# Pooled attention and MLP on one core: keys tiled by head pair, with the leftovers in 32-column matmul tiles

## The chip, the cores and the metric

The kernel runs on one core of a Trainium2 chip. The metric is the device time of one execution in microseconds. Before the change the median of 6 runs is 308.84 us (308.72 to 309.54).

A core has engines that run side by side, each through its own list of instructions in order: TensorE (PE; its weight loads are listed as PEld), VectorE (DVE), ScalarE (ACT), GpSimd (POOL) and SyncE (SP), which here issues transfers only. ACT and POOL issue transfers too. All transfers share 16 DMA engines. TensorE writes its results to PSUM, from which DVE and ACT copy them to the on-chip memory SBUF.

## What is computed

Eight batches of eight heads, 576 tokens, head size 64. Keys and values are averaged over groups of 8 tokens, so a head has 72 pooled keys; the attention output of all heads, 512 wide, goes through an MLP with 2048 hidden units.

```python
batch, n_heads, seq, head_dim = (8, 8, 576, 64)
n_tokens, d_model, d_ff = (4608, 512, 2048)

def _attn_ref(q, k, v):
    pool = 8
    Sp = S // pool                                   # 72
    k_p = k.reshape(B, H, Sp, pool, D).mean(axis=3)
    v_p = v.reshape(B, H, Sp, pool, D).mean(axis=3)
    scores = scale * np.matmul(q, k_p.transpose(0, 1, 3, 2))
    scores = scores - np.max(scores, axis=-1, keepdims=True)
    attn = np.exp(scores)
    attn = attn / (np.sum(attn, axis=-1, keepdims=True) + 1e-09)
    return np.matmul(attn, v_p).astype(np.float32)

def _moe_ref(x, w_in, w_out):
    h = x @ w_in
    g = h - np.tanh(h)
    return (g @ w_out).astype(np.float32)
```

## The kernel before

The order of work is written out by hand: every engine runs its instructions in the order in which the program issues them, and waits where an input is not there yet.

**Keys.** The 8 x 72 = 576 pooled rows of a batch (all heads) are cut into tiles of 128 rows: four full ones and one of 64 (`NT = 5`). `load_rows` (L96) loads tiles 0 to 3 in one transfer on SP and the last in another. `pool_k` (L171) sums each row's 8 tokens in three additions, 8 to 4, 4 to 2, 2 to 1, and writes the sum twice, side by side, into `kd`. `k_transpose` (L212) turns `kd` with matmuls against the identity; because the sum stands there twice, a head's keys appear on partitions 0 to 63 and again on 64 to 127. They are copied into `KB`, which holds for each of the four head pairs a block of all 5 x 128 key columns: an even head on partitions 0 to 63, an odd head on 64 to 127, zeros elsewhere. A tile of 128 rows holds parts of two or three heads, so its scores need the sum over the one or two pairs that it touches (`PAIRS`, L242): 8 matmuls for 5 tiles, or 16 in the two halves of 288 tokens of `scores` (L244). `scores_wide` (L269) does 512 tokens at once, `scores_tail` (L278) the last 64. ACT takes the exponential into `E`.

**Values.** `pool_v` (L193) sums values and multiplies them by a mask into `VB`, with three slots per tile for the heads that the tile may touch; a 65th column per slot gives the softmax's denominator. `av_half` (L296) multiplies `E` by `VB` for four heads: three matmuls of 130, 195 and 65 columns (`XM`, L264) into one PSUM tile `x_ps`; DVE takes the reciprocal of the denominators and multiplies (L311, L312) into `x_sb`. `x_pe_transpose` (L335) turns that on TensorE into `xT`; from batch 2 on a transfer on SP does it (L329).

**MLP.** Tokens go in 9 groups of 512. Per group 16 units of `mlp_h` (four matmuls L380, tanh on ACT L391, subtraction on DVE L393), then 16 units of `mlp_o` (four matmuls L408 each). The attention of batch g+1 is put between the `mlp_o` units of group g: `k_transpose` after unit 0, scores after units 1 to 5, `x_ps` after units 7, 8, 9, 10 and 12. POOL does `pool_k`, `pool_v` and the cast of q ahead of it; SP loads the batch after that while unit 3 of `mlp_h` runs.

**Start (batch 0).** SP loads k in three pieces (tiles 0 and 1, tile 4, tiles 2 and 3), ACT issues q's, POOL v's as bf16 into `v_bf` and then the weights `w1b` (four pieces) and `w2b`. `k_turn` (L547) and `v_pe_pool` (L586) are batch 0's own forms: DVE sums the keys, TensorE sums the values by eight accumulating matmuls against the identity. `warm_pe(n)` puts n spare matmuls into TensorE's list. `av_half` runs for heads 0 to 3 of all four token blocks and then for heads 4 to 7.

**Batch 1** stands between the `mlp_o` units u of group 0 (L679 to L701): `k_transpose` after u = 0, q's transposes from u = 3, scores after u = 4 to 8, `x_ps` after u = 9 to 13, and the transpose of each block (`pend`) one unit after its own `x_ps`. The load of its k waits for the second piece of `w1b` (`after(load_k(1), w1_dmas[1])`), and POOL sums its keys and values.

Of the kernel before, what the change touches and what calls it, by code (L numbers as in the profile page):

```python
# [15 lines left out]
POOL = 8  # L16
# [12 lines left out]
D1 = D + 1  # L29
SCALE = 1.0 / (POOL * float(D) ** 0.5)  # L30
# [3 lines left out]
def kernel(  # L34
# [28 lines left out]
    v_rows = v.rearrange("b h (g j) d -> b (h g) (j d)", j=POOL)  # L63

# [4 lines left out]
    mask = const.tile([128, NT, 3, 1], FP32, name="mask")  # L69
    k_raw = [const.tile([128, NT, POOL * D], FP32, name=f"k_raw{i}") for i in range(2)]  # L70
    v_raw = [const.tile([128, NT, POOL * D], FP32, name=f"v_raw{i}") for i in range(2)]
    KBW = NT * 128
    STEP = KBW + 2 * G
    KB = [const.tile([128, NHP * KBW + 2 * G + KBW], BF16, name=f"KB{i}") for i in range(2)]
    q_bf = const.tile([128, R + 1, H, D], BF16, name="q_bf")
    warm = const.tile([128, 1], FP32, name="warm")
    VB = [const.tile([128, NT, 3, D1], BF16, name=f"VB{i}") for i in range(2)]
# [18 lines left out]
    def load_rows(src, dst, b, t0, t1):  # L96
        if t1 <= 4:
            return nc.sync.dma_start(
                out=dst[:, t0:t1, :],
                in_=src[b, t0 * 128 : t1 * 128, :].rearrange("(t p) n -> p t n", p=128),  # L100
            )
        return nc.sync.dma_start(out=dst[0:64, 4, :], in_=src[b, 512:576, :])

    def load_k(b, cuts=(0, 4, 5)):
        return [load_rows(k_rows, k_raw[b % 2], b, a, z) for a, z in zip(cuts, cuts[1:])]

    def load_v(b, cuts=(0, 4, 5)):
        return [load_rows(v_rows, v_raw[b % 2], b, a, z) for a, z in zip(cuts, cuts[1:])]
# [84 lines left out]
    def pool_v(b, eng, t0=0, t1=NT):  # L193
        r = v_raw[b % 2].rearrange("p t (j d) -> p t j d", d=D)[:, t0:t1, :, :]
        n = t1 - t0
        eng.tensor_tensor(  # L196
            out=r[:, :, 0:4, :], in0=r[:, :, 0:4, :], in1=r[:, :, 4:8, :], op=ALU.add
        )
        eng.tensor_tensor(  # L199
            out=r[:, :, 0:2, :], in0=r[:, :, 0:2, :], in1=r[:, :, 2:4, :], op=ALU.add  # L200
        )
        eng.tensor_tensor(
            out=r[:, :, 0, :], in0=r[:, :, 0, :], in1=r[:, :, 1, :], op=ALU.add
        )
        return eng.tensor_tensor(  # L205
            out=VB[b % 2][:, t0:t1, :, 0:D],
            in0=r[:, :, 0:1, :].to_broadcast([128, n, 3, D]),
            in1=mask[:, t0:t1, :, :].to_broadcast([128, n, 3, D]),
            op=ALU.mult,
        )  # L210

    def k_transpose(b, alloc):  # L212
        kd = kdups.pop(b)
        kb = KB[b % 2]
        for half in range(2):
            ps = alloc([128, 2, 2, G], FP32, "kT_ps")
            flat = ps.rearrange("p i a g -> p (i a g)")
            c = half * 4 * G
            while c < (half + 1) * 4 * G:
                t = c // 128  # L220
                n = min((t + 1) * 128, (half + 1) * 4 * G) - c
                nc.tensor.matmul(  # L222
                    flat[:, c - half * 4 * G : c - half * 4 * G + n],
                    lhsT=kd[:, t, :, :].rearrange("p a d -> p (a d)"),
                    rhs=ident[:, c - t * 128 : c - t * 128 + n],
                    start=True,
                    stop=True,
                )
                c += n
            step = KBW + 2 * G  # L230
            for par, eng in ((0, nc.vector.tensor_copy), (1, nc.scalar.copy)):
                off = 2 * half * step + par * G
                pr = slice(par * D, (par + 1) * D)
                eng(  # L234
                    out=kb[pr, off : off + 2 * step].rearrange("p (i x) -> p i x", x=step)[
                        :, :, 0:G
                    ],
                    in_=ps[pr, :, par, :],
                )

    E_tiles = {}
    PAIRS = [[0], [0, 1], [1, 2], [2, 3], [3]]  # L242

    def scores(b, t):  # L244
# [3 lines left out]
        qT = qTs[b]  # L248
        hs = S // 2
        for half in range(2):  # L250
            ps = ps_a.tile([128, hs], FP32, name="s_ps", tag="ps_a")
            for n, hp in enumerate(PAIRS[t]):
                nc.tensor.matmul(  # L253
                    ps[:, :],
                    lhsT=KB[b % 2][:, hp * KBW + t * 128 : hp * KBW + (t + 1) * 128],
                    rhs=qT[:, hp, half * hs : (half + 1) * hs],
                    start=(n == 0),
                    stop=(n == len(PAIRS[t]) - 1),
                )
# [3 lines left out]

    XM = [  # L264
        [(0, 1, 3, 0), (1, 0, 3, 1), (2, 0, 1, 3)],
        [(2, 1, 3, 0), (3, 0, 3, 1), (4, 0, 1, 3)],
    ]
# [9 lines left out]

    def scores_tail(b):  # L278
# [7 lines left out]
    def score_mms(b, t, dst, c0, c1):  # L286
        for n, hp in enumerate(PAIRS[t]):
            nc.tensor.matmul(  # L288
                dst,
                lhsT=KB[b % 2][:, hp * KBW + t * 128 : hp * KBW + (t + 1) * 128],  # L290
                rhs=qTs[b][:, hp, c0:c1],
                start=(n == 0),
                stop=(n == len(PAIRS[t]) - 1),
            )

    def av_half(b, blk, half, x_sb, alloc):  # L296
# [4 lines left out]
        for n, (t, s0, s1, h0) in enumerate(XM[half]):  # L301
            nc.tensor.matmul(  # L302
                ps[:, h0 : h0 + s1 - s0, :].rearrange("p h d -> p (h d)"),
                lhsT=E[:, t, c0 : c0 + 128],
                rhs=vb[:, t, s0:s1, :].rearrange("p h d -> p (h d)"),
                start=(n == 0),
                stop=(n == 2),
                skip_group_check=True,
            )
# [175 lines left out]
    def load_q0(h0, h1):  # L485
# [5 lines left out]
    load_rows(k_rows, k_raw[0], 0, 0, 2)  # L491
    load_q0(0, 4)
    load_rows(k_rows, k_raw[0], 0, 4, 5)
    load_rows(k_rows, k_raw[0], 0, 2, 4)
    load_q0(4, 8)
    nc.scalar.dma_start(out=t0[:QT, :, R, :], in_=q[0, :, QA:S, :].rearrange("h p d -> p h d"))

    nc.vector.memset(zeros, 0.0)
    warm_pe(13)
    nc.vector.memset(warm[:, :], 0.0)  # L500
    nc.scalar.activation(out=warm[:, :], in_=warm[:, :], func=ACT.Exp)
    nc.vector.memset(k_raw[0][64:128, 4, :], 0.0)
# [3 lines left out]
    nc.gpsimd.memset(v_bf[64:128, 4, :], 0.0)  # L506
    nc.gpsimd.memset(q_bf[64:128, R, :, :], 0.0)
    nc.gpsimd.memset(mask[:, :, :, :], 1.0)
    mflat = mask.rearrange("p t s o -> p t (s o)")
    nc.gpsimd.affine_select(  # L510
        out=mflat,
        in_=mflat,
        compare_op=ALU.is_ge,
        fill=0.0,
        base=G,
        pattern=[[-16, NT], [-G, 3]],
        channel_multiplier=1,
    )
    nc.gpsimd.affine_select(
        out=mflat,  # L520
        in_=mflat,
        compare_op=ALU.is_ge,
        fill=0.0,
        base=-1,
        pattern=[[16, NT], [G, 3]],
        channel_multiplier=-1,
    )
    for i in range(2):
        nc.gpsimd.tensor_scalar_mul(VB[i][:, :, :, D:D1], mask[:, :, :, :], float(POOL))
    nc.gpsimd.dma_start(  # L530
        out=v_bf[:, 0:3, :], in_=v_rows[0, 0:384, :].rearrange("(t p) n -> p t n", p=128)
    )
    nc.gpsimd.dma_start(out=v_bf[:, 3, :], in_=v_rows[0, 384:512, :])
# [235 lines left out]
```

The softmax here doesn't subtract the row's maximum and nothing guards it: scores larger than these inputs give would overflow.

## Time and profile before

| | |
|---|---|
| median of 6 runs | 308.84 us |
| the profiled execution | 308.91 us |
| its span, first to last instruction | 307.2 us |
| TensorE clock granted, mean | 0.998 |
| PE busy | 295.9 us, of it L408 132.7 and L380 126.1 |
| PE, scores of batches 2 to 7 (L253) | 16.7 us, 96 matmuls |
| PE, attention times values (L302) | 21.1 us, 240 matmuls |
| transfers | 48.74 MB, 159 GB/s |

The profile is one execution. Engine times are busy times; they overlap, so they don't add up to the span. A matmul's record runs from its start to its modelled end and holds the pipeline's latency, so a row of records can add up to more than the time in which they were started; the pace is the distance from start to start. An idle time in brackets, "0.30 <-DVE x_sb L312", says how long an engine stood idle before a row and what ended the wait. Some matmul records are missing, so counts in a row can be a little low.

### The profile page before, as it was taken

The page shows a single profiled execution, that of the slowest core. Times are in us where ns is not written, and L with a number is a line of the kernel's source. Part 1 is how long each engine was busy: PE and PEld are TensorE (multiplying, and loading weights), DVE is VectorE, ACT ScalarE, POOL GpSimd, SP SyncE. Part 2 cuts the span into 40 slices and gives each one's busy share as a digit, 9 for nine tenths or more (in the row PEclk, how much of TensorE's full clock was granted, in tenths as well). Part 3 has the DMA queues.
Part 4 walks back from the last instruction along what each step waited for, and adds up shares of the span by engine and source line. Part 5 has one row for each costly group of instructions (what it writes and reads, how often), then busy time and mean ns, then how long its engine had stood idle before and what let it go on. Part 6 is the DMA issues. An engine that isn't in the chain of part 4 may idle for free.

```text
span 307.2 us, 4683 instructions
## 1 busy us (share of the span) xinstructions
PE 295.9 (96%) x1674; PEld 149.1 (49%) x1707; DVE 159.6 (52%) x350; ACT 148.5 (48%) x289; POOL 123.5 (40%) x91
## 2 busy tenths in 40 slices
PE   7889999999999999999999999999999999999995
PEld 2454455445544455445544554455445544444443
DVE  6658714684448524861577066707472657207700
ACT  1757544466336642665166506651566247226511
POOL 8800996870694029700990079208910000000000
PEclk9999999999999999999999999999999999999999
DMA  7999999849754984499557954894521340011033
GB/s 231 233 216 308 247 204 320 254 107 313 187 109 102 299 231 113 97 258 253 104 111 199 325 121 119 217 291 110 112 60 36 82 99 2 34 68 34 3 65 72
DMA packets 61799, 48.74 MB, mean 159 GB/s; under 512 B 35536, under 2 KB 48656, under 8 KB 61776
## 3 DMA queue, kind: packets, MB, share of 16 engines
q1 hardware_dynamic: 55184, 42.35, 51.5%
q0 software_dynamic: 4848, 4.78, 9.4%
q10 hardware_dynamic: 1744, 1.31, 1.5%
q8 instruction: 13, 0.21, 0.3%
q14 instruction: 10, 0.08, 0.1%
HBM read 36.70 MB, written 9.44 MB: 150 GB/s over the span
## 4 chain that ended last, share of the span: by engine, by line
PE 89%; DVE 4%; DMA 3%; issue 1%; ACT 1%; POOL 1%; SPq 0%
PE hT_ps L380 38%; PE o_ps L408 37%; PE x_ps L302 4%; PE s_ps L253 4%; DMA k_raw<-in_k_dram 3%; DVE x_sb L312 2%; DVE gT L393 1%; PE o_ps L429 1%; PE s_ps L288 1%; PE xT_ps L342 1%; PE kT_ps L222 1%; DVE rden L311 1%; POOL kd L185 1%; PE qT_ps L150 0%; ACT t_sb L391 0%
## 5 line engine op out<-in xcount | busy, mean ns | idle before, releaser
L408 PE MATMUL o_ps<-w2b,gT 128*128 128x512 bf16 x541 | 132.7, 379 | 0.8
L393 DVE TENSOR_TENSOR gT<-hT_ps,t_sb 128x512 bf16<-128x512 f32 x144 | 98.9, 691 | 59.1 <-ACT t_sb L391 58.3
L380 PE MATMUL hT_ps<-xT,w1b 128*128 128x512 bf16 x563 | 126.1, 379 | 1.6 <-ACT xT L349 0.5
L391 ACT ACTIVATE t_sb<-hT_ps 128x512 f32<-128x512 f32 x144 | 85.6, 598 | 39.2 <-PE hT_ps L380 38.7
L380 PEld LDWEIGHTS <-w1b 128*128 128x128 bf16 x576 | 56.0, 98 | 67.1 <-issue 1.4
L408 PEld LDWEIGHTS <-gT 128*128 128x128 bf16 x560 | 51.6, 98 | 49.4
L417 ACT COPY o_sb<-o_ps 128x512 f32<-128x512 f32 x33 | 19.3, 586 | 75.6 <-PE o_ps L408 71.6
L311 DVE RECIPROCAL rden<-x_ps 128x4 f32<-128x4 f32 x80 | 14.1, 177 | 59.2 <-PE x_ps L302 58.6
L128 POOL CAST q_bf<-q_raw 128x2048 bf16<-128x2048 f32 x7 | 13.2, 1893 | 78.6 <-DMA q_raw<-in_q_dram 78.6
L312 DVE TENSOR_TENSOR x_sb<-x_ps,rden 128x256 bf16<-128x256 f32 x80 | 33.9, 424 | 2.8
L177 POOL TENSOR_TENSOR k_raw<-k_raw 128x1280 f32<-128x1280 f32 x7 | 20.2, 2889 | 17.8 <-DMA k_raw<-in_k_dram 17.8
L260 ACT ACTIVATE E<-s_ps 128x288 bf16<-128x288 f32 x60 | 21.4, 409 | 9.6 <-PE s_ps L253 9.6
L302 PE MATMUL x_ps<-VB,E 128*128 128x130 bf16 (+2 forms) x240 | 21.1, 221 | 0.1
L302 PEld LDWEIGHTS <-E 128*128 128x128 bf16 x240 | 17.1, 98 | 8.0 <-issue 0.3
L196 POOL TENSOR_TENSOR v_raw<-v_raw 128x1280 f32<-128x1280 f32 x7 | 20.3, 2904 | 0.0
L253 PE MATMUL s_ps<-qT,KB 128*128 128x288 bf16 x96 | 16.7, 287 | 0.0
L253 PEld LDWEIGHTS <-KB 128*128 128x128 bf16 x96 | 9.2, 98 | 9.1 <-ACT KB L234 2.6
L205 POOL TENSOR_TENSOR VB<-v_raw,mask 128x960 bf16<-128x960 f32 x7 | 12.6, 1797 | 0.5
L199 POOL TENSOR_TENSOR v_raw<-v_raw 128x640 f32<-128x640 f32 x7 | 10.8, 1541 | 0.6
L180 POOL TENSOR_TENSOR k_raw<-k_raw 128x640 f32<-128x640 f32 x7 | 10.8, 1537 | 0.6
L185 POOL TENSOR_TENSOR kd<-k_raw 128x640 bf16<-128x640 f32 x7 | 10.8, 1538 | 0.5
L479 PE MATMUL warm_ps<-xT 128*128 128x512 bf16 x28 | 9.6, 466 | 1.3 <-DVE warm L500 1.3
(67 smaller groups left out, 106.7 us busy)
## 6 DMA issues: line engine op xcount, KB each, us to landing
k_raw<-in_k_dram SPq DMA_DIRECT2D x7, 1024.0 KB, 6.7
q_raw<-in_q_dram SPq DMA_DIRECT2D x7, 1024.0 KB, 12.2
v_raw<-in_v_dram SPq DMA_DIRECT2D x7, 1024.0 KB, 10.1
out_dram<-o_sb SPq DMA_DIRECT2D x38, 128.0 KB, 2.4
out_dram<-o_sb SPq DMA_DIRECT2D x16, 256.0 KB, 2.7
w1b<-in_moe_w_in_dram POOLq DMA_DIRECT2D x4, 512.0 KB, 12.5
w2b<-in_moe_w_out_dram POOLq DMA_DIRECT2D x4, 512.0 KB, 6.5
k_raw<-in_k_dram SPq DMA_DIRECT2D x2, 512.0 KB, 6.3
```

The costliest lines, as they stand in the source:

```text
L177: first = eng.tensor_tensor(out=r[:, :, 0:4, :], in0=r[:, :, 0:4, :], in1=r[:, :, 4:8, :], op=ALU.add)
L196: eng.tensor_tensor(out=r[:, :, 0:4, :], in0=r[:, :, 0:4, :], in1=r[:, :, 4:8, :], op=ALU.add)
L253: nc.tensor.matmul(ps[:, :], lhsT=KB[b % 2][:, hp * KBW + t * 128 : hp * KBW + (t + 1) * 128], rhs=qT[:, hp, half * hs : (half + 1) * hs], ...
L260: nc.scalar.activation(out=E[:, t, half * hs : (half + 1) * hs], in_=ps[:, :], func=ACT.Exp, scale=SCALE)
L302: nc.tensor.matmul(ps[:, h0 : h0 + s1 - s0, :].rearrange("p h d -> p (h d)"), lhsT=E[:, t, c0 : c0 + 128], rhs=vb[:, t, s0:s1, :].rearrang ...
L311: nc.vector.reciprocal(out=rden[:, :, :], in_=ps[:, :, D:D1])
L312: nc.vector.tensor_tensor(out=x_sb[:, half, :, :], in0=ps[:, :, 0:D], in1=rden[:, :, :].to_broadcast([128, 4, D]), op=ALU.mult,)
L380: nc.tensor.matmul(h_tiles[i][:, :], lhsT=w1b[:, fb, i * 128 : (i + 1) * 128], rhs=xT[:, fb, tok0 : tok0 + TG], start=(fb == 0), stop=(fb ...
L391: nc.scalar.activation(out=t_sb[:, :], in_=h_ps[:, :], func=ACT.Tanh)
L393: nc.vector.tensor_sub(out=gT[:, :], in0=h_ps[:, :], in1=t_sb[:, :])
L408: nc.tensor.matmul(o_ps[:, :], lhsT=gts[i][:, tb * 128 : (tb + 1) * 128], rhs=w2b[:, i, :], start=(i == 0), stop=(i == NHID - 1),)
L417: (nc.vector.tensor_copy if g == 0 and tb % 2 else nc.scalar.copy)(out=o_sb[:, :], in_=o_ps[:, :])
```

## The change

Rows are now cut by head pair: a pair has 2 x 72 = 144 rows (`PR`), of which the first 128 make a tile (tiles 0 to 3, one per pair) and the last 16 (`LO`) are left over. The four pairs' leftovers share tile 4, pair m on partitions 32m to 32m+15, the other 16 of each 32 staying zero. `KB` shrinks to four blocks of 160 columns (`KP`): 72 of the even head, 56 and 16 of the odd head, 16 of zeros.

```diff
+PR = 2 * G
+LO = PR - 128
+KP = 160
+NM = 4
...
+    k_pairs = k_rows.rearrange("b (t r) n -> b r t n", r=PR)
+    v_pairs = v_rows.rearrange("b (t r) n -> b r t n", r=PR)
...
-    KB = [const.tile([128, NHP * KBW + 2 * G + KBW], BF16, name=f"KB{i}") for i in range(2)]
+    KB = [const.tile([128, NM * KP], BF16, name=f"KB{i}") for i in range(2)]
...
-    VB = [const.tile([128, NT, 3, D1], BF16, name=f"VB{i}") for i in range(2)]
+    VB = [const.tile([128, 3 * NM, D1], BF16, name=f"VB{i}") for i in range(2)]
```

A load of k or v is one transfer of the four full tiles and four of 16 rows, in place of two.

```diff
+    def load_main(src, dst, b, t0, t1):
+        return nc.sync.dma_start(out=dst[:, t0:t1, :], in_=src[b, 0:128, t0:t1, :])
+
+    def load_left(src, dst, b):
+        return [
+            nc.sync.dma_start(out=dst[32 * t : 32 * t + LO, NM, :], in_=src[b, 128:PR, t, :])
+            for t in range(NM)
+        ]
```

`pool_v`'s last multiplication becomes two: `v_main` (128 x 512 elements, two slots per tile) and `v_left` (128 x 256, one slot per head pair's two heads). `k_transpose` makes five matmuls of 128 columns; the copies into `KB` are `kb_main` (DVE takes the even heads of all pairs, ACT the odd ones) and `kb_left` (DVE).

```diff
     def k_transpose(b, alloc):
         kd = kdups.pop(b)
...
+        ps = alloc([128, NM, 128], FP32, "kT_ps")
+        for t in range(NM):
+            turn_tile(ps[:, t, :], kd, t)
+        kb_main(KB[b % 2], ps, 0, NM, (nc.vector.tensor_copy, nc.scalar.copy))
+        ps = alloc([128, 128], FP32, "kT_ps")
+        turn_tile(ps[:, :], kd, NM)
+        kb_left(KB[b % 2], ps, nc.vector.tensor_copy)
```

Scores: a full tile needs its own pair alone, one matmul. The leftover tile needs four, each with 32 columns of weights and its own 32 partitions of PSUM.

```diff
+    def score_mms(b, t, dst, c0, c1, pairs=range(NM)):
+        for m in pairs if t == NM else (t,):
+            o = m * KP + (128 if t == NM else 0)
+            w = 32 if t == NM else 128
+            p = 32 * m if t == NM else 0
+            nc.tensor.matmul(
+                dst[p : p + w],
+                lhsT=KB[b % 2][:, o : o + w],
+                rhs=qTs[b][:, m, c0:c1],
+                start=True,
+                stop=True,
+            )
...
+    def scores_left(b, half):
+        ps = ps_any([128, QA], FP32, "s_ps")
+        score_mms(b, NM, ps, 0, QA, (2 * half, 2 * half + 1))
+        r = slice(64 * half, 64 * half + 64)
+        nc.scalar.activation(out=E_tiles[b][r, NM, 0:QA], in_=ps[r, :], func=ACT.Exp, scale=SCALE)
```

`scores` issues the matmuls of both halves and then both exponentials. `av_half` has three matmuls of 130 columns, the third into every second head's place; with `own=True` (batch 0, blocks 0 to 3) the third reads only the 64 partitions of its own two pairs.

```diff
-        for n, (t, s0, s1, h0) in enumerate(XM[half]):
+        for n in range(3):
+            t = 2 * half + n if n < 2 else NM
+            s0 = 2 * t if n < 2 else 2 * NM + 2 * half
+            r = slice(64 * half, 64 * half + 64) if own and n == 2 else slice(0, 128)
             nc.tensor.matmul(
-                ps[:, h0 : h0 + s1 - s0, :].rearrange("p h d -> p (h d)"),
-                lhsT=E[:, t, c0 : c0 + 128],
-                rhs=vb[:, t, s0:s1, :].rearrange("p h d -> p (h d)"),
+                ps[:, 2 * n : 2 * n + 2, :].rearrange("p h d -> p (h d)")
+                if n < 2
+                else ps.rearrange("p (a s) d -> p a s d", s=2)[:, :, 1, :],
+                lhsT=E[r, t, c0 : c0 + 128],
+                rhs=vb[:, s0 : s0 + 2, :].rearrange("p h d -> p (h d)")
+                if n < 2
+                else vb[r, s0 : s0 + 2, :],
```

The start: loads in smaller pieces and another order, two memsets ahead of the leftovers' loads, v's leftovers loaded by SP into the idle `v_raw[1]` and cast by POOL, the sums of the k leftovers on POOL. Four selects build the mask in place of two.

```diff
-    load_rows(k_rows, k_raw[0], 0, 0, 2)
-    load_q0(0, 4)
-    load_rows(k_rows, k_raw[0], 0, 4, 5)
-    load_rows(k_rows, k_raw[0], 0, 2, 4)
-    load_q0(4, 8)
+    nc.vector.memset(zeros, 0.0)
+    nc.vector.memset(k_raw[0][:, NM, :], 0.0)
+    nc.vector.memset(v_raw[1][:, NM, :], 0.0)
+    load_main(k_pairs, k_raw[0], 0, 0, 1)
+    load_q0(0, 2)
+    load_main(k_pairs, k_raw[0], 0, 1, 2)
+    load_q0(2, 4)
+    load_left(k_pairs, k_raw[0], 0)
+    load_q0(4, 8)
+    load_main(k_pairs, k_raw[0], 0, 2, 4)
+    load_left(v_pairs, v_raw[1], 0)
...
-    nc.gpsimd.dma_start(out=v_bf[:, 3, :], in_=v_rows[0, 384:512, :])
-    nc.gpsimd.dma_start(out=v_bf[0:64, 4, :], in_=v_rows[0, 512:576, :])
-    for c in range(4):
-        load_w1(c)
+    nc.gpsimd.dma_start(out=v_bf[:, 0:NM, :], in_=v_pairs[0, 0:128, :, :])
+    pool_k(0, nc.gpsimd, NM, NT)
+    load_w1(0)
+    load_w1(1)
+    nc.gpsimd.tensor_copy(out=v_bf[:, NM, :], in_=v_raw[1][:, NM, :])
+    load_w1(2)
+    load_w1(3)
     load_w2(0)
```

The order of batch 0's work, with v summed in one piece and the leftover scores of heads 0 to 3 apart from those of heads 4 to 7:

```diff
-    q_turn(nc.vector.tensor_copy, 0, 4)
-    k_turn(0, 2)
+    q_turn(nc.scalar.copy, 0, 2)
+    q_turn(nc.scalar.copy, 2, 4)
+    k_turn(0, 1)
+    q_pe_transpose(0, (0,), "act")
     warm_pe(1)
-    q_pe_transpose(0, (0, 1), "act")
-    pool_k(0, nc.vector, 4, 5)
+    k_turn(1, 2)
+    q_pe_transpose(0, (1,), "act")
+    warm_pe(2)
+    scores_wide(0, (0, 1))
+    q_turn(nc.scalar.copy, 4, 6)
+    warm_pe(2)
+    k_turn_left()
     pool_k(0, nc.vector, 2, 4)
+    q_turn(nc.vector.tensor_copy, 6, 8)
+    warm_pe(1)
+    scores_left(0, 0)
     warm_pe(3)
-    scores_wide(0, (0, 1))
-    q_turn(nc.scalar.copy, 4, 8)
-    warm_pe(5)
-    k_turn(2, 5)
+    k_turn(2, 4)
     q_pe_transpose(0, (2, 3), "act")
-    v_pe_pool(0, 3)
-    scores_wide(0, (2,))
-    v_pe_pool(3, 5)
-    scores_wide(0, (3, 4))
+    v_pe_pool()
+    warm_pe(1)
+    scores_wide(0, (2, 3))
+    scores_left(0, 1)
```

Ahead of it `warm_pe(13)` becomes `warm_pe(9)`. In batch 1 the transposes of `x_sb` follow their `x_ps` by two units instead of one:

```diff
-    pend = None
+    pend = []
...
         if u >= 9:
-            if pend is not None:
-                x_pe_transpose(1, *pend)
-                pend = None
+            if u >= 11 and pend:
+                x_pe_transpose(1, *pend.pop(0))
             if u <= 13:
-                pend = (u - 9, av(1, u - 9, ps_any, False))
+                pend.append((u - 9, av(1, u - 9, ps_any, False)))
```

## The prediction

> **What bounds the kernel now.** I read the page first, then a table of busy time by stretch, then instructions in order of time around three places where TensorE waits.
>
> ```profile
> span 307.2 us, 4683 instructions
> PE 295.9 (96%) x1674; PEld 149.1 (49%) x1707; DVE 159.6 (52%) x350; ACT 148.5 (48%) x289; POOL 123.5 (40%) x91
> ...
> PE 89%; DVE 4%; DMA 3%; issue 1%; ACT 1%; POOL 1%; SPq 0%
> ```
> ```profile
> 57.70:296.00 238.30, 236.93 (x1277) 118.12 (x1302) 125.31 (x261) 117.17 (x229) 86.67 (x51) 1.00 0.53 139
> ```
> The second fence is one stretch: bounds, length, then busy time of PE, PEld, DVE, ACT, POOL, clock, DMA. Between 57.7 and 296 us PE is busy 236.9 of 238.3, so there a removed PE slot is removed from the end. Outside it other things end waits. The run's own time is 308.91, 1.71 above its span, and 0.07 above the median of 308.84; I sum against 308.91 and subtract 0.07 last.
>
> Steady batches, rows in order of time (start, length, engine, line):
> ```profile
> 72.34 0.43 PE L222 MATMUL kT_ps<-ident,kd 128*128 128x128 bf16 x6
> 72.61 1.02 PE L408 MATMUL o_ps<-w2b,gT 128*128 128x512 bf16 x4
> 73.57 0.42 PE L253 MATMUL s_ps<-qT,KB 128*128 128x288 bf16 x2
> ...
> 74.69 0.65 PE L253 MATMUL s_ps<-qT,KB 128*128 128x288 bf16 x4
> 75.18 1.03 PE L408 MATMUL o_ps<-w2b,gT 128*128 128x512 bf16 x4
> ```
> ```profile
> 73.56 0.17 PEld L253 LDWEIGHTS <-KB 128*128 128x128 bf16 x2 [0.43 <-ACT KB L234]
> ```
> Lengths hold pipeline latency; the pace is start to start: 75.18 - 74.69 = 0.49 for four, 0.1225 us per 288-column matmul. Four L408 matmuls take 0.86, so the first scores could start at 72.61 + 0.86 = 73.47; they start at 73.57: 0.10 lost to the KB copy.
>
> The start and batch 1:
> ```profile
> 13.67 0.47 PEld L589 LDWEIGHTS <-ident 128*128 128x128 bf16 x8 [0.30 <-DMA v_raw<-in_v_dram]
> 15.23 0.52 PE L302 MATMUL x_ps<-VB,E 128*128 128x130 bf16 x6
> ...
> 29.35 0.39 PE L288 MATMUL s_ps<-qT,KB 128*128 128x64 bf16 x8
> ```
> ```profile
> 35.31 1.56 POOL L185 TENSOR_TENSOR kd<-k_raw 128x640 bf16<-128x640 f32 x1
> ...
> 36.92 0.29 PEld L222 LDWEIGHTS <-kd 128*128 128x128 bf16 x6 [0.61 <-POOL kd L185]
> ...
> 46.29 1.80 POOL L205 TENSOR_TENSOR VB<-v_raw,mask 128x960 bf16<-128x960 f32 x1
> ...
> 48.14 0.52 PE L302 MATMUL x_ps<-VB,E 128*128 128x130 bf16 x6
> ...
> 49.75 0.11 PEld L342 LDWEIGHTS <-x_sb 128*128 128x128 bf16 x2 [0.30 <-DVE x_sb L312]
> ```
> See three gates: v of batch 0 must land (13.6) before attention; batch 1's K transpose waits for POOL (kd ends 36.87, PE was free at 35.78 + 0.86 = 36.64); batch 1's first x_ps waits for POOL's VB (ends 48.09, PE free at 47.94). POOL works from 30.05 to 48.09 without a pause, started by k of batch 1 landing (28.6 and 29.9), whose load waits for w1's second piece (18.6). So a faster batch 0 gains at most some 0.3; a slower one is paid. (Landings are issue times plus the times to landing.)
>
> **Steady part (batches 2 to 7).** Per batch now: scores 16 x 0.1225 = 1.96; wait 0.10; K transpose 72.61 - 72.34 = 0.27; x_ps ten halves at 0.18 (48.14 to 48.49 holds two) = 1.80. After: tiles 0 to 3 take one pair each, 8 x 0.1225 = 0.98. K transpose is 5 x 0.056 = 0.28, and its copies (one DVE, one ACT, then 64x64) end within the 0.86 of L408, so the 0.10 goes; without that cover it comes back. x_ps has 390 columns per half as before: 1.77 to 1.80. The leftover tile is 8 matmuls of 32 columns of weights, a form no row shows. Low end: four work side by side, two in a row on each quarter, 2 x 0.1225 + 3 starts of 0.029 (eight L288 matmuls of 64 columns: 0.39 less the 0.19 of one, over seven) = 0.33. High end: one after another, 0.98 (rival 3 lies beyond). A switch into and out of such tiles may empty the array: 0 to 0.165 each (0.19 latency less 0.029 pace). I take side by side, as the L288 row is the nearest: small matmuls whose starts do not wait for earlier ends (their records overlap sixfold); and 0.08, the middle, per switch: 0.33 + 0.16 = 0.49, bounds 0.33 and 1.31. Saving 1.96 + 0.10 - 0.98 - 0.49 - 0.01 + 0.02 = 0.60 a batch, times 6 = **-3.6** (bounds -4.6 and +1.3).
>
> [...]
>
> SP gets 12 load issues a batch in place of 6, 0.5 to 0.6 each (L102: 0.52 to 0.58): 3.3 us more. Queued behind them are q's load and, in batch 2, the stores. q's DMA sits behind k and v in one queue anyway (k, v, q of batch 3 land at 72.2, 75.9, 79.6), and its cast on POOL comes at the end of the group; without that slack up to 3 us would fall on PE. POOL's VB multiplies shrink from 960 to 512 + 256 elements, -0.3 by length. Nothing.
>
> **Batch 1, transposes two steps late.** Now each x transpose follows its own x_ps by one step and waits for DVE. Five times: xT halves start at 49.35 and 49.75 although two matmuls take 0.11: 0.29, 0.29, 0.29, 0.29 and 0.34 (the 64-column one) = 1.50. Two steps later, DVE (two halves of 0.18 + 0.42, 1.2 per step) keeps under PE's step of 0.86 + 0.36 + 0.22 = 1.44; PSUM has three buffers in turn, and each is copied before its third use. **-1.5**; if DVE sets the step, -1.2.
>
> **Start and the two POOL gates.** SP issues k tiles 0, 1, four leftovers (from about 1.9, behind two 0.48 memsets), then tiles 2 to 3 at about 4.2 instead of 1.94. ACT's q pieces pass it. SP and ACT move 2.36 MB by 10.3 now and 0.13 more then, so it lands at 10.4 to 10.8 and the v leftovers near 11. POOL issues v at about 4.0 (one memset of 0.52 gone, two selects of 0.23 more), then its wait for the k leftovers (landed 8.0 now) stands ahead of w1's issues: three additions of about 0.6, 0.3, 0.3 give w1 at 9 to 10; queued behind are the v leftover cast (0.5) and w1's second half. v's data fill the software queue until 13.3, so w1 is not late; that cover ends if w1 issues after about 11. On PE the leftovers' transpose, on DVE its copy wait for the same POOL sums; behind them stand DVE's sums of tiles 2 and 3, which wait for their load until 10.4 anyway. ACT's extra exp (0.60) falls where it waits for PE.
>
> DVE adds a 0.45 q cast ahead of KB's copies; it lies under v's landing. v in one 512 KB piece lands at 13.3 to 13.7; one sum of 8 x 0.136 = 1.09, then a spare 0.22, two scores 0.43, leftover 0.22 to 0.43 with switches 0.16, spares 0.43: x_ps at 15.9 to 16.3 instead of 15.23, +0.8. Eight halves then each mix 64-row and 128-row tiles: PE's 0.51 per half (0.18, a spare 0.216, 0.11) plus two switches (0.16) exceeds DVE's 0.59 by 0.08 in some: +0.4 (bounds 0 and 2). PE comes to batch 1's K transpose at 36.64 + 1.2 = 37.8, against 36.93: **+0.9**. Then batch 1: scores 8 x 0.216 become 4 x 0.216 + 0.30 + 0.16, -0.40; the tail's leftover brings two more switches, +0.16; -0.24. x_ps comes at 47.94 + 0.9 - 0.24 = 48.6 (VB's gate, 47.8, no longer binds) against 48.14: **+0.5** in all (-0.3 to +2.3).
>
> **Sum.** 308.91 + 0.5 - 1.5 - 3.6 = 304.3; less 0.07, **304.2**. Own range 302.6 to 306.2.
>
> **Rivals.**
> 1. Narrow tiles run one after another at 0.1225. For: all read the same 128 rows of weights. Against: their columns are disjoint. Batch 1 +0.56 (four of 0.216 against 0.30), steady 6 x (0.98 - 0.33) = +3.9: 308.7.
> 2. The start falls further back: leftovers of 32 KB land late, POOL holds w1, k of batch 1 and kd follow. For: 11 SP issues, POOL waits in order. Against: the queues are full until 13 us anyway. 2 us late: 306.2.
> 3. Slower: every narrow matmul also pays the emptying of the array, 0.1225 + 0.165 = 0.29, in the score stage of each batch. 6 x (2.30 - 0.33) = +11.8, batch 1 4 x 0.381 - 0.30 = +1.2: 304.2 + 13.0 = 317.2. It decides from about 0.14 us per tile (eight tiles at 0.33 + 4.7/6 = 1.1). For: only small or full-array rows exist here, so nothing rules it out. Against: the overlap of the L288 records.
>
> **How the numbers follow.** Forecast 0.62, rival 1 0.11, rival 2 0.12, rival 3 0.15. Under 0.2% (0.6 us) a measurement of this kernel cannot tell from no change. Rival 1 is on that edge: 0.09 same, 0.02 slower. Faster 0.74, same 0.09, slower 0.17. The range goes from 302.5 (switches and start cheap) to 308.3, which leaves out rivals 3 and most of 1.
>
> **What would show it.** Steady leftover block: from its first matmul to the next L408, 0.33 to 0.55 us confirms; about 1.0 is rival 1; over 1.3 is rival 3. Batch 1: no DVE wait ahead of xT, step 1.44 instead of 1.74. Start: v lands by 13.7, x_ps by 16.3, w1's second piece by 19, batch 1's K transpose by 38; later ones are rival 2. I am wrong if the stretch from batch 2 to the last group shortens by under 2 us, or if PE waits there for KB or qT.

## The result and the profile after

The changed kernel is slower, not faster: 310.28 us (median of 20 runs, 309.31 to 311.98) against 308.92 (median of 41 runs, 308.36 to 309.81); ratio 1.0046 [1.0036, 1.0055]. The forecast was 304.2, and its range ended at 308.3. The profiled execution took 310.33 us, with a span of 308.6 against 307.2. One single execution of all the runs below, one of e10's five, took 1769.92 us and is left out of e10's interval.

The page of the changed kernel, the rows that answer to those of before, and the row of the granted clock (tenths of full speed in 40 slices):

```profile
span 308.6 us, 4718 instructions
PE 295.0 (96%) x1657; PEld 144.6 (47%) x1689; DVE 159.7 (52%) x349; ACT 148.5 (48%) x285; POOL 120.0 (39%) x100
...
PEclk9789999999999999999999999999999999999999
...
PE 86%; DMA 5%; DVE 4%; ACT 3%; issue 1%; ACTq 0%; SPq 0%
```

The chain of waits has moved: PE's share fell from 89% to 86%, DMA's rose from 3% to 5%, ACT's from 1% to 3%, and the clock row has a dent in its first slices. The stretch of before, read again (PE, PEld, DVE, ACT, POOL, clock, DMA):

```profile
57.70:296.00 238.30, 236.11 (x1294) 114.92 (x1319) 128.75 (x269) 118.64 (x228) 89.19 (x60) 1.00 0.57 144
```

PE is still busy 236.1 of 238.3 us there: what follows the start is still bound by PE. So I cut both executions at the same three events of PE, the first `x_ps` of batch 0, the first of batch 1, and the first `mlp_h` matmul of group 1:

| stretch | before | after | difference | forecast |
|---|---|---|---|---|
| start of the span to first x_ps of batch 0 | 15.23 | 19.85 | +4.62 | +0.8 |
| from there to first x_ps of batch 1 | 32.91 | 33.10 | +0.19 | -0.3 |
| from there to group 1 | 9.53 | 8.10 | -1.43 | -1.5 |
| from there to the end of the span | 249.5 | 247.5 | -2.0 | -3.6 |
| sum | 307.2 | 308.6 | +1.4 | -4.6 |

The loss is in the first 20 us. The steady part gains 1.6 less than forecast. Batch 1's late transposes bring what they should. The second row is 0.5 over its forecast; no run follows that up, but it is 33.1 us in every run that has the changed kernel's start, and 32.9 in e5, as before the change.

The start, instructions of the changed kernel in order of time:

```profile
6.05 0.41 SPq L101 DMA_DIRECT2D k_raw<-in_k_dram  x1
...
10.28 0.72 POOL L186 TENSOR_TENSOR k_raw<-k_raw 128x256 f32<-128x256 f32 x1 [5.63 <-DMA k_raw<-in_k_dram]
...
12.12 0.29 PE L247 MATMUL kT_ps<-ident,kd 128*128 128x128 bf16 x1 [3.50 <-POOL kd L194]
...
13.24 0.69 DVE L186 TENSOR_TENSOR k_raw<-k_raw 128x512 f32<-128x512 f32 x1 [0.57 <-DMA k_raw<-in_k_dram]
...
16.24 2.26 PE L596 MATMUL v_ps<-v_raw,ident 128*128 128x320 bf16 x8
...
19.85 0.44 PE L327 MATMUL x_ps<-VB,E 128*128 128x130 bf16 x3
```

Read down: the load of k tiles 2 and 3 is issued at 6.05, where I had 4.2, and lands at 13.22 (issue plus its time to landing), where I had 10.4 to 10.8 and before it was 10.32. DVE starts to sum them in that moment. PE stands for 3.50 us until POOL has summed the leftovers. Behind it the eight matmuls that sum v start at 16.24. All data of v had landed by 13.99, and POOL's cast of the leftovers ended at 14.85, but PE's list puts the sums behind the transpose of tiles 2 and 3. Their row is 2.26 us long; by the starts they take 2.14 where I had 1.09.

Why 6.05? The waits of SP's own queue in the first 20 us (total, times, longest) name q:

```profile
SPq L105 <- DMA q_raw<-in_q_dram: 2.9, 2, 1.7
SPq L101 <- DMA q_raw<-in_q_dram: 0.9, 1, 0.9
```

SP issues no load of q there, and before the change the same view has no such wait. In the trace the fifteen transfers of SP and ACT report their landing on eight counters (semaphores 100, 102 and 104 to 109) in turn, so the ninth has 100 again, and it is issued when the first has landed. The times agree to 0.02 us. Counted by counters, k tiles 2 and 3 are the eleventh, issued at 6.05, and the third, q heads 2 and 3, landed at 6.04. The ninth, a leftover, was issued at 4.38, and the first, q heads 0 and 1, landed at 4.36; the thirteenth, a leftover of v, went at 8.12, and the fifth, q heads 4 to 7, landed at 8.10. Before the change the start has six such transfers, in the change fifteen.

Why 2.26? Two stretches of the changed kernel (length, then PE, PEld, DVE, ACT, POOL, clock, DMA):

```profile
9.00:12.00 3.00, 0.00 (x0) 0.00 (x0) 0.00 (x0) 0.40 (x1) 1.56 (x3) 0.91 1.13 297
```
```profile
11.46:18.29 6.83, 5.74 (x25) 2.68 (x26) 3.28 (x7) 1.66 (x3) 6.13 (x11) 0.50 0.92 167
```

PE did nothing from 9 to 12 us, and from 11.46 to 18.29 the granted clock was 0.50. The sums of v were started every 0.267 us there, against 0.135 at full clock (in e11 below). The clock fell when PE had stood still for 2.85 us, from 8.61 on. The stretch of 6.83 is twice 3.41, the length of single ones in e9 and e11; the last section has the figures of other runs.

Batch 1 and the steady part, in order of time:

```profile
52.95 0.51 PE L327 MATMUL x_ps<-VB,E 128*128 128x130 bf16 x6
...
61.05 1.24 PE L409 MATMUL hT_ps<-xT,w1b 128*128 128x512 bf16 x5
```
```profile
76.21 0.81 PE L437 MATMUL o_ps<-w2b,gT 128*128 128x512 bf16 x3
76.29 0.44 DVE L237 CAST KB<-kT_ps 64x288 bf16<-64x288 f32 x1
...
76.77 0.34 ACT L238 CAST KB<-kT_ps 64x224 bf16<-64x224 f32 x1 [1.11 <-DVE KB L237]
...
77.16 0.42 PE L272 MATMUL s_ps<-qT,KB 128*128 128x288 bf16 x2
...
80.74 1.03 PE L437 MATMUL o_ps<-w2b,gT 128*128 128x512 bf16 x4
...
81.70 0.43 PE L272 MATMUL s_ps<-qT,KB 128*32 128x288 bf16 x8
...
82.06 0.61 PE L437 MATMUL o_ps<-w2b,gT 128*128 128x512 bf16 x2
```

First the copies of the keys: DVE's ends at 76.73, and ACT's begins only then. The two don't run side by side, although they read different partitions; so the scores start at 77.16, which is 0.30 after the matmuls ahead of them (76.21 + 0.65 for the three of the row). Then the leftover block: eight 32-column matmuls between 81.60 (80.74 + 0.86) and 82.06, 0.46 us in all, 0.10 of it before the first. The second four start 0.13 after the first, at 81.83; with 0.12 for them, some 0.10 is left behind the last.

### The profile page after: what moved, and what is told of

The parts are those of the page before. It is cut to its first block, busy times and chain, and to the rows that moved or that the text cites. A ratio compares the mean times of both kernels' runs of the same rounds, so it can differ in the third digit from the quotient of the medians.

```text
span 308.6 us, 4718 instructions
## 1 busy us (share of the span) xinstructions
PE 295.0 (96%) x1657; PEld 144.6 (47%) x1689; DVE 159.7 (52%) x349; ACT 148.5 (48%) x285; POOL 120.0 (39%) x100
## 4 chain that ended last, share of the span: by engine, by line
PE 86%; DMA 5%; DVE 4%; ACT 3%; issue 1%; ACTq 0%; SPq 0%
PE hT_ps L409 39%; PE o_ps L437 36%; PE x_ps L327 5%; PE s_ps L272 4%; DVE gT L422 3%; DMA k_raw<-in_k_dram 2%; ACT t_sb L420 2%; DMA q_raw<-in_q_dram 2%; DMA out_dram<-o_sb 1%; PE xT_ps L371 1%; DVE KB L237 1%; ACT KB L238 1%; PE v_ps L596 1%; PE warm_ps L508 1%; PE qT_ps L159 1%
## 5 line engine op out<-in xcount | busy, mean ns | idle before, releaser
L437 PEld LDWEIGHTS <-gT 128*128 128x128 bf16 x560 | 52.3, 98 | 50.4 <-issue 1.4
L186 POOL TENSOR_TENSOR k_raw<-k_raw 128x1280 f32<-128x1280 f32 (+1 forms) x8 | 20.9, 2613 | 24.6 <-DMA k_raw<-in_k_dram 24.6
L327 PE MATMUL x_ps<-VB,E 128*128 128x130 bf16 (+1 forms) x240 | 21.8, 221 | 0.0
L327 PEld LDWEIGHTS <-E 128*128 128x128 bf16 (+1 forms) x240 | 17.2, 97 | 9.1
L272 PE MATMUL s_ps<-qT,KB 128*128 128x288 bf16 (+5 forms) x128 | 17.4, 293 | 0.9
L272 PEld LDWEIGHTS <-KB 128*32 128x32 bf16 (+1 forms) x128 | 7.0, 96 | 13.2 <-issue 3.8
L189 POOL TENSOR_TENSOR k_raw<-k_raw 128x640 f32<-128x640 f32 (+1 forms) x8 | 11.2, 1402 | 0.6
L194 POOL TENSOR_TENSOR kd<-k_raw 128x640 bf16<-128x640 f32 (+1 forms) x8 | 11.2, 1403 | 0.6
L207 POOL TENSOR_TENSOR v_raw<-v_raw 128x640 f32<-128x640 f32 x7 | 10.8, 1542 | 0.5
L378 ACT CAST xT<-xT_ps 128x256 bf16<-128x256 f32 (+1 forms) x14 | 6.1, 434 | 7.8 <-PE xT_ps L371 7.6
```

The costliest lines, as they stand in the source:

```text
L186: first = eng.tensor_tensor(out=r[:, :, 0:4, :], in0=r[:, :, 0:4, :], in1=r[:, :, 4:8, :], op=ALU.add)
L272: nc.tensor.matmul(dst[p : p + w], lhsT=KB[b % 2][:, o : o + w], rhs=qTs[b][:, m, c0:c1], start=True, stop=True,)
L327: nc.tensor.matmul(ps[:, 2 * n : 2 * n + 2, :].rearrange("p h d -> p (h d)") if n < 2 else ps.rearrange("p (a s) d -> p a s d", s=2)[:, :, ...
L437: nc.tensor.matmul(o_ps[:, :], lhsT=gts[i][:, tb * 128 : (tb + 1) * 128], rhs=w2b[:, i, :], start=(i == 0), stop=(i == NHID - 1),)
```

## The experiments

Each was compared with the kernel before, run beside it on the same chip (medians there 308.78 to 308.81). "The change" below is the changed kernel, 310.28, which was measured beside 308.92; so a distance from it is good to some 0.1 us. Theory A: the start's loss comes from where loads wait and from the half clock, the steady part's shortfall from the serial copies. The rivals are those on record with each run.

**e1, the kernel before with the late transposes of batch 1 alone.**

```diff
-            if pend is not None:
-                x_pe_transpose(1, *pend)
-                pend = None
+            if u >= 11 and pend:
+                x_pe_transpose(1, *pend.pop(0))
...
```

> The kernel before with one part of the change: batch 1's x transposes two units after their x_ps. Theory (this part gave 1.4 us of the changed kernel): the five waits for DVE ahead of xT (0.29 to 0.34 each) go, a unit takes 1.44 instead of 1.74 us, and the median falls by 1.3 to 1.5 us, to about 307.5. Rival (the faster units run into DVE or a PSUM buffer): under 0.6 us.

307.34 us, 0.9949 [0.9936, 0.9962]: -1.44.

```profile
47.83 0.52 PE L302 MATMUL x_ps<-VB,E 128*128 128x130 bf16 x6
...
55.94 6.42 PE L380 MATMUL hT_ps<-xT,w1b 128*128 128x512 bf16 x29
```

From the first `x_ps` of batch 1 to group 1 it is 8.11 us against 9.53, with no wait for `x_sb` left. The term is right.

**e2, the change with k tiles 2 and 3 loaded ahead of the leftovers**, and the leftovers' transpose behind DVE's sums of those tiles.

```diff
+    load_main(k_pairs, k_raw[0], 0, 2, 4)
+    load_q0(4, 8)
     load_left(k_pairs, k_raw[0], 0)
-    load_q0(4, 8)
-    load_main(k_pairs, k_raw[0], 0, 2, 4)
...
-    k_turn_left()
     pool_k(0, nc.vector, 2, 4)
     q_turn(nc.vector.tensor_copy, 6, 8)
+    k_turn_left()
```

> The changed kernel with the load of k tiles 2 and 3 of batch 0 issued ahead of the leftovers' loads, and their sums on DVE ahead of the leftovers' copy. Theory (eight counters serve all transfers of SP and ACT in turn, so that the ninth and later wait for an earlier one to land): the load is issued by 2.7 us instead of 6.05 and lands by 11 instead of 13.2; the start gains 0.5 to 1.5 us. Rival (bandwidth: the bytes take their time in any order): it lands at 13 again and the time stays within 0.3 us.

311.29 us, 1.0074 [1.0058, 1.0089]: slower by 1.0 than the change. The load was issued at 1.72 and landed at 9.27, as theory A said. But the leftovers now landed at 9.97 to 12.46 and v at 14.45, the leftovers' transpose, which PE's list still puts first, ran at 14.55, the sums of v began at 18.06, and the clock was at 0.50 again from 11.54 to 18.36. The wait went to the transfers behind: the thirteenth was issued at 11.20, when the fifth by counters, q heads 4 to 7, landed at 11.19. My time was wrong, a miss: I had followed one transfer, not the last of the set.

**e3, the change with 15 spare matmuls in place of 2 in PE's first pause.**

```diff
-    warm_pe(2)
+    warm_pe(15)
     k_turn_left()
```

> The changed kernel with 15 instead of 2 spare matmuls in the pause of 3.5 us ahead of the leftovers' transpose. Theory (the pause halves TensorE's clock, and the half clock costs time until 18 us): the clock stays at 1.0 from 12 to 19 us, the eight sums of v take about 1.15 us from first to last instead of 2.26, first x_ps of batch 0 by 18.7 instead of 19.85, and the time falls by 1.0 to 1.6 us, to about 309. Rival (loads and POOL set the start, the clock is cover): under 0.4 us.

310.95 us, 1.0053 [1.003, 1.0077]: no gain, a miss. In the profiled execution the clock fell at the next pause instead (0.50 from 16.1 to 19.51). Its seven runs tell more: three with a mean granted clock of 0.999 or more took 309.55 to 309.68, the other four, at 0.989 to 0.994, 310.95 to 312.10. The half clock goes with 1.3 us or more, and one pause filled doesn't keep it away in every run.

**e4, the change with the weights issued ahead of POOL's sums of the leftovers.**

```diff
+    for c in range(4):
+        load_w1(c)
+    load_w2(0)
     pool_k(0, nc.gpsimd, NM, NT)
-    load_w1(0)
-    load_w1(1)
...
```

> The changed kernel with POOL issuing w1 and w2's first piece ahead of its sums of the k leftovers. Theory (POOL's hold of w1 is covered, as TensorE comes late to batch 1's K transpose in any case): w1's second piece lands by 19.2 instead of 19.94, batch 1's kd ends 0.7 us or more earlier than 39.52, and the time stays within 0.4 us. Rival (the hold of w1 sets the start): 1.0 us or more faster.

313.25 us, 1.0124 [1.0099, 1.0149]: 3 us slower than the change; neither the theory nor the rival had that. The second piece of w1 landed at 19.25 instead of 19.94, and the sums of batch 1's keys ended at 37.52 instead of 39.52, as the rival wanted. But DVE's start on k tiles 2 and 3 went back from 13.24:

```profile
14.52 0.69 DVE L186 TENSOR_TENSOR k_raw<-k_raw 128x512 f32<-128x512 f32 x1 [0.87 <-DMA k_raw<-in_k_dram]
```

Their load was issued at 5.77, 0.28 earlier than in the change, and landed 1.28 later. The clock was at 0.50 from 12.13 to 22.37, the first `x_ps` came at 22.96, and batch 1's K transpose at 45.34, long after its keys. So the late weights of the change cost nothing; that they kept the way clear for batch 0's loads is how I read the later landing.

**e5, the change with batch 0 started as before**: k tiles 0 and 1 in one load, q in two, the loads of k tiles 2 and 3 as eighth transfer of SP and ACT, v's leftovers through POOL as bf16, all sums of keys on DVE, no 64-row tiles.

```diff
-    load_main(k_pairs, k_raw[0], 0, 0, 1)
-    load_q0(0, 2)
-    load_main(k_pairs, k_raw[0], 0, 1, 2)
-    load_q0(2, 4)
+    load_main(k_pairs, k_raw[0], 0, 0, 2)
+    load_q0(0, 4)
...
-    load_left(v_pairs, v_raw[1], 0)
...
-    pool_k(0, nc.gpsimd, NM, NT)
...
+    for t in range(NM):
+        nc.gpsimd.dma_start(
+            out=v_bf[32 * t : 32 * t + LO, NM, :], in_=v_pairs[0, 128:PR, t, :]
+        )
```

> The changed kernel (its tiles, its narrow leftover tile, its batch 1) with batch 0 started as in the kernel before: k tiles 0 and 1 in one load, q in two, all sums of k on DVE, v's leftovers loaded as bf16 by POOL, w1 issued after them, no 64-row tiles, heads not apart. Theory (the loss lies in the start alone, and the rest of the change is worth about 3.3 us: 1.4 in batch 1 and 0.31 in each of six batches): batch 0's first x_ps by 16.3 us instead of 19.85, clock 1.0 throughout, median 305.2 to 306.8. Rival (the new tiles make any start late, since the leftovers are small loads): 308.5 or more.

307.06 us, 0.9942 [0.9928, 0.9956]: 3.2 under the change, 0.26 over the expected range.

```profile
13.69 1.25 PE L593 MATMUL v_ps<-v_raw,ident 128*128 128x320 bf16 x8 [1.13 <-DMA v_raw<-in_v_dram]
...
16.07 0.28 PE L327 MATMUL x_ps<-VB,E 128*128 128x130 bf16 x2
```

Three of its six runs kept the clock (0.997 or more) and took 306.49 to 306.67, inside that range; the others, at 0.992 to 0.994, 307.46 to 307.81. k tiles 2 and 3 landed at 10.05, and group 1 began at 57.08. With the late transposes and an unchanged start group 1 would have begun at 57.66 - 1.43 = 56.23; so this start costs +0.85 where the change's costs 61.05 - 56.23 = +4.8. The leftovers are small loads here too, so the rival is out.

**e6, e5 with the K transposes in two PSUM tiles**, one copied by DVE alone, the other by ACT alone.

```diff
-        ps = alloc([128, NM, 128], FP32, "kT_ps")
-        for t in range(NM):
-            turn_tile(ps[:, t, :], kd, t)
-        kb_main(KB[b % 2], ps, 0, NM, (nc.vector.tensor_copy, nc.scalar.copy))
+        for t0, eng in ((0, nc.vector.tensor_copy), (2, nc.scalar.copy)):
+            ps = alloc([128, 2, 128], FP32, "kT_ps")
+            for t in range(2):
+                turn_tile(ps[:, t, :], kd, t0 + t)
+            kb_main(KB[b % 2], ps, t0, t0 + 2, (eng, eng))
```

> e5_old_start with the four K transposes of a batch in two PSUM tiles, one copied by DVE and one by ACT, instead of one that DVE and ACT copy one after the other. Theory (PE waits 0.30 us per batch for KB because the two copies do not run side by side): the wait ahead of the first scores falls from 0.30 to under 0.10 and the time by 1.0 to 1.7 us against e5_old_start. Rival (the copies are slow in themselves): under 0.4 us.

305.03 us, 0.9876 [0.9863, 0.9889], the best measured: 1.5 under e5's runs at full clock. In order of time:

```profile
72.15 0.27 ACT L237 CAST KB<-kT_ps 64x144 bf16<-64x144 f32 x1 [0.49 <-PE kT_ps L247]
72.30 0.29 DVE L237 CAST KB<-kT_ps 64x144 bf16<-64x144 f32 x1
...
72.94 0.42 PE L273 MATMUL s_ps<-qT,KB 128*128 128x288 bf16 x2
```

The copies now overlap, and PE reaches the scores 0.08 after its four matmuls (started at 72.00) where e5 has 0.31. Six batches at 0.23 are 1.4 us, and from group 1 to the end the two profiles differ by as much (247.67 and 246.32). Theory A holds for the steady part.

**e7, e5 with the leftover scores as four accumulated matmuls of full width**, over zero-padded keys.

```diff
...
-                dst[p : p + w],
-                lhsT=KB[b % 2][:, o : o + w],
+                dst,
+                lhsT=kx,
                 rhs=qTs[b][:, m, c0:c1],
-                start=True,
-                stop=True,
+                start=t < NM or m == 0,
+                stop=t < NM or m == NM - 1,
```

> e5_old_start with the leftover tile's scores in full-width matmuls: the leftovers' keys in zero-padded blocks of 128 columns, four matmuls summed into one PSUM tile. Theory (narrow tiles run side by side; entering and leaving them costs about 0.1 each): the block takes 8 x 0.1225 = 0.98 us instead of 0.46, six batches and batch 1 make 2.8 to 3.7 us more than e5_old_start. Rival (narrow tiles save nothing): within 0.5 us.

309.84 us, 1.0031 [1.0019, 1.0043]: 2.8 over e5's median, 3.3 over its runs at full clock. The block:

```profile
77.89 1.14 PE L271 MATMUL s_ps<-qT,KL 128*128 128x288 bf16 x8
...
78.86 1.46 PE L436 MATMUL o_ps<-w2b,gT 128*128 128x512 bf16 x6
```

Eight matmuls take 0.97 us, so the narrow form (0.46) saves 0.5 a batch, 3.1 in six (from group 1 to the end it is 250.75 here, 247.67 in e5). Rivals 1 and 3 of the prediction are out.

**e8 and e10, the change with spare matmuls in both pauses** (15 and 12; 15 and 7).

```diff
-    warm_pe(2)
+    warm_pe(15)
     k_turn_left()
...
-    warm_pe(3)
+    warm_pe(7)
     k_turn(2, 4)
```

> The changed kernel with 15 instead of 2 spare matmuls ahead of the leftovers' transpose and 12 instead of 3 behind the first leftover scores, so that both pauses are filled. Theory (e3 filled one pause of two, so the clock fell all the same): the clock stays 1.0 until v is summed, the eight sums take 1.1 us instead of 2.1, first x_ps 1.3 to 2.3 us earlier than in the changed kernel for the same load times, time 308.0 to 309.3. Rival (loads and POOL set the start): within 0.5 us of the changed kernel.

> e8 with 7 instead of 12 spare matmuls in the second pause, as 12 ran past the arrival of the K sums and delayed the transpose of tiles 2 and 3. Theory (the half clock costs about 1 us of the start): the clock stays 1.0, K transpose of tiles 2 and 3 by 15.4, first x_ps by 18.7 for load times like the changed kernel's, time 309.0 to 309.5. Rival (no clock loss on the path): 310 or more.

e8: 310.04 us, 1.005 [1.0032, 1.0069], a miss: the profiled execution kept the clock, but twelve spares ran past the arrival of the keys, and the transpose of tiles 2 and 3 started at 16.13 instead of 15.20. Nor is the clock safe with both pauses filled: two of its nine runs, at 0.994, took 311.83 and 311.93. e10: 309.99 us, 1.0036 [1.0023, 1.0049], with the clock at 1.00, but over its range of 309.0 to 309.5. Its loads came as late as e3's (k tiles 2 and 3 at 14.07 and 13.97), so e3 and e10 show the clock's price. The sums of v in e3, then in e10:

```profile
17.00 2.34 PE L596 MATMUL v_ps<-v_raw,ident 128*128 128x320 bf16 x8
```
```profile
16.94 1.25 PE L596 MATMUL v_ps<-v_raw,ident 128*128 128x320 bf16 x8
```

The first `x_ps` comes at 20.84 in e3 and at 19.53 in e10: 1.3 us. Against the change, e8 and e10 gain no more than 0.3 us: the late loads remain.

**e11, the change with fewer transfers ahead of k tiles 2 and 3, and nothing else**: k tiles 0 and 1 in one load, q heads 0 to 3 in one, q's tail on SP at the end. The load becomes the eighth.

```diff
-    load_main(k_pairs, k_raw[0], 0, 0, 1)
-    load_q0(0, 2)
-    load_main(k_pairs, k_raw[0], 0, 1, 2)
-    load_q0(2, 4)
+    load_main(k_pairs, k_raw[0], 0, 0, 2)
+    load_q0(0, 4)
...
-    nc.scalar.dma_start(out=t0[:QT, :, R, :], in_=q[0, :, QA:S, :].rearrange("h p d -> p h d"))
+    nc.sync.dma_start(out=t0[:QT, :, R, :], in_=q[0, :, QA:S, :].rearrange("h p d -> p h d"))
```

> The changed kernel with k tiles 0 and 1 in one load, q's heads 0 to 3 in one, and q's last tokens on SP at the end, so that k tiles 2 and 3 are the eighth transfer and need no counter of an earlier one. Nothing else is touched. Theory (waiting for counters made that load late): it is issued by 4 us instead of 6.05 and lands by 10.6 instead of 13.2, the leftovers land by 9.1; x_ps by 18 instead of 19.85, time 308.0 to 309.2. Rival (order and number of transfers do not matter, the bytes do): load at 13, time 310 or more.

307.43 us, 0.9956 [0.9944, 0.9968]: 2.85 under the change.

```profile
3.86 0.44 SPq L101 DMA_DIRECT2D k_raw<-in_k_dram  x1
...
14.31 1.25 PE L594 MATMUL v_ps<-v_raw,ident 128*128 128x320 bf16 x8 [0.19 <-POOL v_raw L560]
...
16.90 0.44 PE L327 MATMUL x_ps<-VB,E 128*128 128x130 bf16 x3
```

The load is issued 2.2 us earlier, right behind the leftovers, and lands at 10.73, inside the 10.4 to 10.8 of the prediction. The first `x_ps` is 2.95 earlier. The ninth transfer waits as the theory of the counters has it: issued at 6.35, after the first, q, landed at 6.27. It gained more than I expected, since the clock changed with it: one stretch at half clock is left in place of two (7.59 to 11.00 in the profile), and the sums of v run at full clock, some 1.05 of the 2.95. Of its five runs one, at 307.09, had the clock at 1.00.

**e9, e6 with the leftover scores ahead of those of tiles 2 and 3** (`scores_wide(0, (4, 2, 3))` for `(2, 3, 4)`).

> e6_old_start_kb_split with batch 0's leftover scores ahead of those of tiles 2 and 3. Theory (in e5 and e6 the first x_ps of batch 0 stops 0.47 us for the exponential of the leftover tile, which came third): that wait goes, batch 1's K transpose comes up to 0.7 us earlier (38.23 before, POOL's kd ends at 37.3), time 304.2 to 304.8. Rival (POOL's VB for batch 1 ends the wait there in any case): within 0.2 us of 305.03.

305.74 us, 0.99 [0.9888, 0.9913]: a miss. Two of its four runs had a clock of 0.993 or 0.994 (306.07 and 306.20), the profiled one with 0.50 from 13.76 to 17.17; the two at 0.998 or more took 305.18 and 305.41, no better than e6. What the order is worth stays open.

**e12, the change without the 64-row tiles of batch 0** (`av_half(..., ps_all)` without `True`).

> The changed kernel without 64-row tiles in batch 0. Two switches per half cost PE about 0.20 us (160 ns in place of 57 twice), so a half takes 0.71 us where DVE needs 0.60; without them the halves keep DVE's pace, but the first one waits for the second leftover exponential, some 0.7 us. Theory (both cancel): within 0.5 us of the changed kernel. Rival (the 64-row tiles made the start late): 1 us or more faster.

310.66 us, 1.0055 [1.004, 1.0071], within 0.4 of the change: the 64-row tiles are neither the loss nor a visible gain.

## Why the prediction was wrong

**The step that failed** is the first of the start: "SP issues k tiles 0, 1, four leftovers ..., then tiles 2 to 3 at about 4.2", hence "it lands at 10.4 to 10.8". I priced a transfer at its issue time, from rows of a trace with only six such transfers, where nothing waits. With fifteen, the eleventh waited for the third to land: issued at 6.05, landed at 13.22. e11 changes no more than the loads: with two merged away and q's tail put last, the load is the eighth, and the wait is gone: the load lands at 10.73, and the time falls by 2.85 us, to the right side of the kernel before. (Of the 2.36 MB that the prediction has landed by 10.3 before the change, q's tail, 0.13, landed at 13.16.)

**The second step that failed** is "one sum of 8 x 0.136 = 1.09": it takes full clock for granted, and the start term put the half clock at nothing without a reason. The sums took 2.14. e3's runs at full and at reduced clock differ by 1.3 us or more, and e3's and e10's profiles by 1.3. The sum of the start: the prediction has the sums of v begin as v lands, 13.3 to 13.7, and `x_ps` at 15.9 to 16.3; they began at 16.24, 2.5 to 2.9 later, and their half clock adds 1.05. That makes 3.6 to 4.0, and `x_ps` at 19.85 is as much behind.

With the wait gone, the start is still not the one on record. e11 has `x_ps` at 16.90 and group 1 at 58.19, which is +1.96 by the reckoning of e5, against +0.5. Its sums of v start at 14.31, right behind POOL's cast of v's leftovers, which landed at 13.49 where I had "near 11": they are the ninth to twelfth transfers there, and wait too. e5, another start, with no such cast and no 64-row tiles, costs +0.85.

**Start, other points.** w1 was issued at 12.00, past the 11 from which I said the cover ends, and its second piece landed at 19.94 (I had 19). It cost nothing: batch 1's keys were summed by 39.52, and PE came to their transpose at 42.23 on its own account. e4 shows the reverse danger. Rival 2 named the right stage, a start that falls back by late leftovers, with a chain over w1 and `kd` that did not bind and half the price. v's 512 KB piece landed at 12.03, earlier than the 13.3 to 13.7 on record, and bought nothing.

**Steady part**, -2.0 for -3.6; by one of the prediction's own signs it is wrong here too, since PE waits for KB. The narrow tiles were sized well: 0.46 measured, 0.49 forecast, side by side. Its two parts, 0.33 and 0.16, came as 0.26 and 0.20, so the sum came closer than its parts, by luck. No run shows that a switch empties the array; the rows show 0.10 on each side. The step that failed is "its copies (one DVE, one ACT, then 64x64) end within the 0.86 of L408, so the 0.10 goes". They run one after the other and the wait grows to 0.30. Six batches at 0.20 more instead of 0.10 less are 1.8 us, of which the narrow tiles give back 0.03 a batch; measured shortfall 1.6. A row of before had shown it, and I had not read its bracket:

```profile
73.24 0.49 ACT L234 CAST KB<-kT_ps 64x144 bf16<-64x144 f32 x2 [0.96 <-DVE KB L234]
```

There too ACT waits for DVE's copy of the same tile; but there were two tiles of half the size, so ACT worked in the first while DVE was in the second, and only one short copy (0.29) stood ahead of it. In the change DVE and ACT read different halves of the partitions of one tile, and this program kept them apart all the same (76.29 to 76.73, then 76.77 to 77.11); in e6, with one tile for each, they overlap (72.30 to 72.59 and 72.15 to 72.42).

**Batch 1**, -1.43 measured twice (here and in e1) against -1.5: right.

**Together:** forecast +0.5 - 1.5 - 3.6, measured +4.8 - 1.4 - 2.0 = +1.4. The eleven SP issues of the start, priced by their lengths alone, decided the sign. e6, with the start nearly as before and the copies side by side, takes 305.03, which is 3.8 under the kernel before. That lies inside the range on record, but it is another kernel than the one forecast.

## What to carry to other kernels

Splitting a load into pieces cost more than issue time here (e11, with two loads merged away and q's tail last, took 2.85 us less): count the transfers in flight, find which one each further transfer waits for, and look in the queue's own waits for transfers of another engine. Before calling two copies parallel, read the bracket of the one that starts second in the trace at hand. Where TensorE is idle in a start, price the clock too (1.3 us between e3 and e10), and follow the last arrival of a set of loads: in e2 moving k tiles 2 and 3 forward, from 13.22 to 9.27, moved POOL's sums of the leftovers back, from 10.28 to 12.72.

## What the runs showed of the hardware

- **The half clock came in whole stretches of 3.41 us.** One in e9 (13.76 to 17.17) and in e11 (7.59 to 11.00), two in the change, three in e4 (12.13 to 22.37). PE need not be idle for it: in the 3.41 us before, it was busy 0.56 us in the change, 0.90 in e9, 1.48 in e11 and 1.74 in e3. e5 kept its clock after 1.61, so no single threshold comes out. The clock came back after 3.41 us with PE busy 2.94 (e12) to 3.41 (e3, e9), and stayed down after 2.44 (e4) and 2.65 (the change). Nor is it the same in every run: one stretch of 3.41 at half clock lowers the mean by 3.41 x 0.5 / 308 = 0.0055, and the 20 runs of the change lie in such steps: five at 0.992 or 0.993 (309.31 to 309.95), thirteen at 0.988 or 0.989 (309.98 to 311.43), two at 0.983 (311.32 and 311.98).
- **The narrow matmuls of the block shown started 3 to 4 ns apart**: 81.699, 81.703, 81.706 and 81.709; the second four came from 81.833 on, 0.134 us after the first. What it cost to enter, 0.10 us, and some 0.10 to leave, are from the rows above.
- **A transfer of 32 KB took 5.3 us from issue to landing** in the crowded start (the change's four leftovers of k, median), against 3.3 for the 256 KB issued just before them.
